# Pooled attention and a soft mixture of experts on one core: fewer and longer idle products on TensorE, one more row group of w2 by halves, and the uneven rows moved from w2 to w1

## The chip, the core and the metric

The kernel runs on one core of one Trainium2 chip. The metric is the device time of one execution in microseconds (us); of several runs of a kernel the median is given. The page and the views quoted below come from one execution taken by the hardware profiler. Its span, from the first to the last instruction, is a little shorter than its time.

## The reference

What is computed is an attention over pooled keys and values, and behind it a soft mixture of experts on the attention's output:

```python
# q, k, v: (8, 8, 576, 64); phi: (512, 32); w1: (8, 512, 1024); w2: (8, 1024, 512); all float32
k_p = k.reshape(B, H, Sp, pool, D).mean(axis=3)         # pool = 8, Sp = 72
v_p = v.reshape(B, H, Sp, pool, D).mean(axis=3)
attn = softmax(scale * np.matmul(q, k_p.transpose(0, 1, 3, 2)))
x = np.matmul(attn, v_p)                                # as (4608, 512)
logits = x @ phi
slot_input = softmax(logits, axis=0).T @ x              # 32 slots, 4 for each of 8 experts
for e in range(E):
    slot_out[e] = np.maximum(slot_input[e] @ w1[e], 0.0) @ w2[e]
out = softmax(logits, axis=1) @ slot_out                # (4608, 512)
```

## The kernel before

The batch is worked in four pairs of two. For each pair the kernel pools k and v with products against a constant matrix, turns q, forms the scores, exponentiates them on ScalarE (ACT) and multiplies by v extended by v times phi, so that x and the logits come out together. These stages are interleaved by hand; each engine runs its instructions in the order in which the code writes them. When the fourth pair is done, the slots' inputs are there, and the experts follow: `hidden()` (w1), `turn_hidden()`, and `second_layer()` (w2, which adds up in one PSUM tile, `so_ps`). Then every tile of 128 rows of the output is one product with `so` (`product()`), scaled by ACT or VectorE (DVE) in `put()` and stored from SyncE (SP) in `store()`.

All inputs but a part of k come in through DMAs that GpSimd (POOL) issues, with a cast from float32 to bfloat16 on the way. POOL issues them in the order in which the code writes them, and the order in which they land is that one: q, k, v of the pairs, with w1 (`load_w1`, L103) between them from the second pair on, then w2 (`load_w2`, L109; L458 and L459), and at last the pieces of L482. Sizes in the views of the DMA are those of the destination, in bfloat16.

Of the experts' w2, experts 0 to 5 are loaded in whole rows. Of expert 6 (`E - 2`) the first `CUT6` = 4 of its 8 row groups (a row group: 128 rows, one on each partition, 512 columns) come in whole rows, 8 KB of float32 on each partition, by L459; this load is cut by partitions into 0 to 112, 112 to 120 and 120 to 128, so that it is three DMAs. The remaining 4 groups of expert 6 and the 8 of expert 7 are loaded by halves of the columns (L477 to L485): first the left 256 columns of all of these groups in the four pieces of `PIECES` (L92), then the right 256 columns. So the left half of the output can be begun (`begin(0)`, L632) before the right half of these weights is there.

While TensorE (PE) waits for w2, it runs products whose result nobody reads: `busy(n)` (L556) writes n products of 512 bfloat16 columns into `idle_ps`. The calls stand at L626 to L631: 6 before expert 6's whole rows, 3 behind them, and 3 and 2 behind the first two pieces of the left half. `row_sums()` (L393) forms the divisors of the output rows with ten products, a copy by ACT, four float32 transposes (L404) and two reciprocals by DVE (L405, L406).

The first product of the left half's output is L586; it needs the last piece of the left half. The output's tiles are stored in groups of 2, 2, 2, 4, 6, 8 and 12 rows on each partition; tiles 0 to 9 by halves of the columns, the last three groups in whole rows of 12, 16 and 24 KB on each partition.

Of the kernel before, what the change touches and what calls it, by code (L numbers as in the profile page):

```python
# [8 lines left out]
FP = mybir.dt.float32  # L9
# [9 lines left out]
def kernel(  # L19
# [10 lines left out]
    nc = tc.nc  # L30
# [4 lines left out]
    DM = H * D  # L35
    E = moe_w1.shape[0]
# [11 lines left out]
    DJ = DM // 128  # L48
    FJ = F // 128
# [21 lines left out]
    xsa = persist.tile([128, 2, 9 * H * XW], BF)  # L71
    exa = persist.tile([128, 2, 2, HQ, 2, S // 2], BF)
    w1_sb = persist.tile([128, E, DJ, F], BF)
    cT = persist.tile([128, 2, B * S // 2], BF)
# [11 lines left out]

    CUT6 = FJ - 4
    HC = DM // 2  # L90
    halves = [slice(0, HC), slice(HC, DM)]
    PIECES = ((E - 2, CUT6, FJ), (E - 1, 0, 4), (E - 1, 4, FJ - 1), (E - 1, FJ - 1, FJ))  # L92

    loaded = 0

    def load(src, pair):
        nonlocal loaded
        loaded += 1
        t = big[:, loaded % 4]
        nc.gpsimd.dma_start(out=t, in_=pair_of(src, pair))  # L100
        return t.rearrange("p (t d) -> p t d", d=D)

    def load_w1(e, n):  # L103
        nc.gpsimd.dma_start(out=w1_sb[:, e:e + n].rearrange("p e j f -> p e (j f)"),
                            in_=moe_w1[e:e + n].rearrange("e (p j) f -> p e (j f)", j=DJ))

    w2_at = {}

    def load_w2(home, e, n, j0=0, j1=FJ, parts=((0, 128),)):  # L109
        for i in range(n):  # L110
            for j in range(j0, j1):
                w2_at[e + i, j] = home[:, i, j * DM:(j + 1) * DM]
        src = moe_w2[e:e + n].rearrange("e (p j) d -> p e j d", j=FJ)[:, :, j0:j1].rearrange("p e j d -> p e (j d)")
        for p0, p1 in parts:
            nc.gpsimd.dma_start(out=home[p0:p1, 0:n, j0 * DM:j1 * DM], in_=src[p0:p1])


    CUT = 4 * POOL * D
# [8 lines left out]
    ident = consts.tile([128, 128], BF)  # L127
# [32 lines left out]
    with tc.tile_pool(name="tmp", bufs=1) as tmp:  # L160
# [39 lines left out]
    def after_k(p):  # L200
        if p + 1 < NP:
            q_sb[p + 1] = load(q, p + 1)
        if p == 1:
            load_w1(0, 1)

    def after_q(p):
        if p + 1 < NP:
            v_sb[p + 1] = load(v, p + 1)
        if p == 1:
            load_w1(1, 1)  # L210
        if p == 2:
# [37 lines left out]
    def prepare_kq(pair):  # L249

        means = kvpool.tile([128, NR, 2, D], BF, name="kmeans")
        yield from pool_stage(k_sb[pair], means, lambda: after_k(pair))
        kp[pair] = kvpool.tile([128, BH, SP], BF, name="kp", bufs=2)
        dst = kp[pair].rearrange("p n (r i) -> p r n i", r=NR)
        yield from turn_stage(means, lambda r0, r1, ps: nc.vector.tensor_copy(out=dst[:, r0:r1], in_=ps))
        for n, t0 in enumerate(range(0, NU, 6)):
            ps = ps_m.tile([128, 6, BH, NI], BF, name="q_ps", tag="m")
            for t in range(6):
                tt = 2 * (t0 + t)
                nc.tensor.transpose(out=ps[:, t].rearrange("p n i -> p (n i)"),  # L260
                                    in_=q_sb[pair][:, tt:tt + 2, :].rearrange("p t d -> p (t d)"), identity=ident)
            dst = qT[pair][:, :, t0:t0 + 6, :].rearrange("p n t i -> p t n i")
            if n % 3 == 1:
                nc.scalar.copy(out=dst, in_=ps)  # L264
            else:
                nc.vector.tensor_copy(out=dst, in_=ps)  # L266
            if n == NU // 6 - 1:
                after_q(pair)
            yield
# [123 lines left out]
    def row_sums():  # L393

        ps = ps_m.tile([NC, 4, 128], FP, name="R_ps", tag="m")
        for c, (_, t) in enumerate(quads + rest):
            nc.tensor.matmul(out=ps[:, 0:2 * t.shape[1]].rearrange("p (s r) i -> p s r i", r=2), 
                             lhsT=onehot[:, MAXC - 1 - c:MAXC - 1 - c + NC], rhs=t,
                             start=(c == 0), stop=(c == NC - 1), skip_group_check=True)
        sums = consts.tile([NC, 4, 128], FP)  # L400
        nc.scalar.copy(out=sums, in_=ps)
        ps = ps_m.tile([128, 4, NC], FP, name="RT_ps", tag="m")
        for i in range(4):
            nc.tensor.transpose(out=ps[:, i], in_=sums[:, i], identity=identf[0:NC, 0:NC])  # L404
        nc.vector.reciprocal(out=recR[:, 0:2], in_=ps[:, 0:2])  # L405
        nc.vector.reciprocal(out=recR[:, 2:4, 0:len(quads)], in_=ps[:, 2:4, 0:len(quads)])  # L406
# [21 lines left out]
    for pair in range(NP):  # L428
        for qd in range(2):
# [24 lines left out]
            if qd == 1:  # L454
                for _ in prep or ():
                    pass
            last = (pair, qd, ex)
    load_w2(qTa, 4, 2)  # L458
    load_w2(xsa[:, 0:1], E - 2, 1, 0, CUT6, ((0, 112), (112, 120), (120, 128)))  # L459

    u_tile(*last[:2], 4, last[2], by_scalar=True)
    G_ps = ps_m.tile([128, DM], FP, name="G_ps", tag="m")
# [6 lines left out]
    def half_home(e, half):  # L469
        if e == E - 1:  # L470
            flat = xsa[:, 1, half * FJ * HC:(half + 1) * FJ * HC]
        else:
            c0 = CUT6 * DM + half * (FJ - CUT6) * HC
            flat = xsa[:, 0, c0:c0 + (FJ - CUT6) * HC]
        return flat.rearrange("p (j c) -> p j c", c=HC)

    w2_half = {}  # L477
    for half, cols in enumerate(halves):
        for e, j0, j1 in PIECES:
            home = half_home(e, half)  # L480
            i = 0 if e == E - 1 else CUT6
            nc.gpsimd.dma_start(out=home[:, j0 - i:j1 - i],  # L482
                                in_=moe_w2[e].rearrange("(p j) d -> p j d", j=FJ)[:, j0:j1, cols])
# [44 lines left out]
    def second_layer(e, j0=0, j1=FJ, half=None):  # L528
        cols = slice(0, DM) if half is None else halves[half]
        for fj in range(j0, j1):  # L530
            g = fj % NG
            nc.tensor.matmul(out=so_ps[g * NS:(g + 1) * NS, cols], lhsT=hT[:, e, fj],  # L532
                             rhs=w2_at[e, fj] if half is None else w2_half[e, fj, half],
                             start=(e == 0 and fj < NG), stop=(e == E - 1 and fj >= NG), skip_group_check=True)
# [18 lines left out]

    idle = ps_m.tile([128, 512], FP, name="idle_ps", tag="m")

    def busy(n):  # L556
        for _ in range(n):
            nc.tensor.matmul(out=idle, lhsT=ident, rhs=cT[:, 0, 0:512], start=True, stop=True)  # L558

    def scaled(engine, dst, src, by):  # L560
        if engine == 0:
# [9 lines left out]
    n = 0  # L571
    places = []
    for rows, base in GROUPS:
        home = out_a[:, n:n + rows] if n + rows <= 6 else out_b[:, n - 6:n - 6 + rows]
# [25 lines left out]
    def begin(half):  # L600

        cols = halves[half]
        scaled(0, so_a[:, cols], so_ps[:, cols], recC)
        f0 = product(0, cols, True)
        second_layer(E - 1, J7, FJ, half)
        f1 = product(1, cols, True)
        put(0, cols, 0, f0)
        store(0, 0, 1, cols)
        scaled(1, so[:, cols], so_ps[:, cols], recC)
        put(1, cols, 0, f1)  # L610
        store(0, 1, 2, cols)
# [9 lines left out]
    for e in range(4):  # L621
        second_layer(e)
    row_sums()
    for e in range(4, E - 2):
        second_layer(e)
    busy(6)  # L626
    second_layer(E - 2, 0, CUT6)
    busy(3)
    for (e, j0, j1), n in zip(PIECES[:-1], (3, 2, 0)):
        second_layer(e, j0, j1, 0)  # L630
        busy(n)  # L631
    begin(0)  # L632
    tiles(2, 3, 0)
    tiles(3, 4, 0)
# [11 lines left out]
    for n in range(10, len(TILES)):  # L646
        g, r = TILES[n]
# [33 lines left out]
```

## Time and profile before

| | us |
|---|---|
| median of 3 runs | 177.48 (177.26 to 177.49) |
| the profiled execution, its time | 177.27 |
| its span | 175.5 |
| PE busy | 126.8 |
| DVE busy | 93.1 |
| ACT busy | 88.0 |
| POOL busy | 19.0 |

How to read the views. In a row of a timeline stand the start, the length, the engine, the line of the code, the operation, output and inputs by the program's names with their shapes, how many instructions the row groups, and in brackets the idle time of the engine before them with what ended it. PEld is TensorE's load of weights, which overlaps its products (PE). `POOLq` and `SPq` are these engines' queues of instructions. A row of windows gives a stretch and its length, then the busy time of PE, PEld, DVE, ACT and POOL with the number of instructions, the share of the clock that the throttle granted TensorE, the mean busy share of the 16 DMA engines by the packets that start in the stretch (over 1 where packets overlap), and the GB/s that they moved, by the destination's size. A row of a DMA queue has packets, MB, and the time of the packets as a share of 16 engines over the stretch asked for. A row of a DMA issue has the size and the median time from issue to landing.

### The profile page before, as it was taken

To read this page: it belongs to the slowest core of one execution; us is meant where nothing else is said; L and a number is where in the kernel's file an instruction comes from. 1 tells how busy PE (TensorE), PEld (TensorE's weight loads), DVE (VectorE), ACT (ScalarE), POOL (GpSimd) and SP (SyncE) were. 2 spreads that over 40 slices of the span, in tenths; PEclk is the share of its full clock that TensorE was granted. 3 is DMA by queue.
4 is the path that set the end of the run, shared out by engine and by line. 5 is a ranking of instruction groups with operands and counts; after the bars stand their busy time and mean duration, and the time that the engine had idled before them with its cause. 6 is when DMAs were issued, how large, how long until landed. Compare 5 with 4: busy or idle time off the path is not lost.

```text
span 175.5 us, 2874 instructions
## 1 busy us (share of the span) xinstructions
PE 126.8 (72%) x1119; PEld 68.9 (39%) x1119; DVE 93.1 (53%) x257; ACT 88.0 (50%) x168; POOL 19.0 (11%) x36
## 2 busy tenths in 40 slices
PE   0005787999899999999999897459968598795000
PEld 0002443665556655556655455323531233331000
DVE  5403344497868588795897758603540005698000
ACT  3201249884987649877399952440201006896000
POOL 7000111022110040000010024003010140000000
PEclk9999999999999999999999997557999789999555
DMA  5999999999999999999999999999999999999991
GB/s 196 245 210 225 218 210 216 220 212 222 207 218 218 211 227 206 220 212 215 220 220 211 213 217 222 215 213 213 222 217 213 196 195 216 309 395 439 463 387 73
DMA packets 10381, 41.14 MB, mean 234 GB/s; under 512 B 752, under 2 KB 6384, under 8 KB 6656
## 3 DMA queue, kind: packets, MB, share of 16 engines
q0 software_dynamic: 7040, 30.48, 85.4%
q1 hardware_dynamic: 3328, 10.49, 15.4%
q8 instruction: 9, 0.15, 0.3%
q14 instruction: 4, 0.03, 0.0%
HBM read 61.93 MB, written 9.44 MB: 407 GB/s over the span
## 4 chain that ended last, share of the span: by engine, by line
PE 35%; DMA 26%; issue 11%; ACT 11%; DVE 7%; POOL 1%; DVEq 0%; ACTq 0%; POOLq 0%
DMA qTa<-in_moe_w_dram 19%; PE pool_ps L228 9%; DMA phi_f<-in_moe_phi_dram 7%; PE q_ps L260 5%; PE sc L300 4%; ACT exa L302 4%; DVE w_sb L564 4%; PE u_ps L314 4%; PE idle_ps L558 2%; ACT vmeans L234 2%; PE G_ps L336 2%; PE so_ps L532 2%; PE turn_ps L244 2%; PE f_ps L589 1%; PE lg_ps L332 1%
## 5 line engine op out<-in xcount | busy, mean ns | idle before, releaser
L302 ACT ACTIVATE exa<-sc 72x576 bf16<-72x576 f32 x64 | 39.4, 653 | 4.6 <-PE sc L300 3.9
L325 DVE TENSOR_TENSOR xsa<-u_ps,rec 128x384 bf16<-128x384 f32 x69 | 37.5, 554 | 1.3
L314 PE MATMUL u_ps<-vp,exa 72*128 72x97 bf16 (+1 forms) x320 | 27.2, 218 | 4.2 <-DVE xsa L325 3.3
L314 PEld LDWEIGHTS <-exa 72*128 72x128 bf16 (+1 forms) x320 | 18.4, 105 | 15.1 <-DVE xsa L325 6.4
L300 PE MATMUL sc<-qTa,kp 64*72 64x288 bf16 x128 | 21.4, 302 | 1.9 <-ACT exa L302 1.5
L228 PE MATMUL pool_ps<-big,pmat 128*128 128x512 bf16 x64 | 18.1, 403 | 0.7 <-ACT qTa L264 0.6
L319 DVE RECIPROCAL rec<-u_ps 128x4 f32<-128x4 f32 x72 | 11.5, 173 | 12.5 <-PE u_ps L314 12.4
L180 PE MATMUL phi_ps<-spread,sel 128*128 128x256 bf16 x4 | 1.3, 394 | 15.0 <-DVE spread L175 15.0
L260 PE MATMUL q_ps<-ident,big 128*128 128x128 bf16 x144 | 11.6, 219 | 0.8 <-DVE qTa L266 0.3
L589 PE MATMUL f_ps<-so,cT 128*128 128x512 bf16 (+1 forms) x42 | 10.2, 337 | 1.8 <-ACT w_sb L562 0.8
L336 PE MATMUL G_ps<-xsa,ee 128*128 128x512 bf16 x36 | 10.2, 438 | 1.2 <-ACT ee L333 1.2
L300 PEld LDWEIGHTS <-kp 64*72 64x72 bf16 x128 | 7.9, 107 | 8.2 <-issue 3.1
L564 DVE TENSOR_SCALAR w_sb<-f_ps,recR 128x512 f32<-128x512 f32 (+1 forms) x17 | 10.5, 681 | 0.3
L236 DVE TENSOR_REDUCE rsum<-rest_ps 128x64 f32<-128x512 f32 x8 | 5.5, 692 | 8.6 <-PE rest_ps L232 8.5
L264 ACT COPY qTa<-q_ps 128x768 bf16<-128x768 bf16 x8 | 6.4, 795 | 7.0 <-PE q_ps L260 7.0
L260 PEld LDWEIGHTS <-big 128*128 128x128 bf16 x144 | 8.7, 97 | 2.9 <-issue 1.3
L562 ACT ACTIVATE w_sb<-f_ps,recR 128x512 f32<-128x512 f32 (+1 forms) x17 | 9.6, 639 | 0.4 <-PE f_ps L589 0.2
L266 DVE COPY qTa<-q_ps 128x768 bf16<-128x768 bf16 x16 | 8.8, 552 | 1.7 <-PE q_ps L260 1.6
L482 POOL DMA_DIRECT2D xsa<-in_moe_w_dram x8 | 5.7, 713 | 30.7 <-PE G_ps L336 11.4
L228 PEld LDWEIGHTS <-pmat 128*128 128x128 bf16 x64 | 5.8, 102 | 6.4 <-issue 2.4
L234 ACT CAST vmeans<-pool_ps 128x1024 bf16<-128x1024 f32 x4 | 4.0, 1012 | 6.8 <-PE pool_ps L228 6.8
L292 ACT CAST vp<-v_ps 72x384 bf16<-72x384 f32 x16 | 7.1, 488 | 0.1
(101 smaller groups left out, 147.4 us busy)
## 6 DMA issues: line engine op xcount, KB each, us to landing
w_sb<-in_moe_w_dram POOLq DMA_DIRECT2D x2, 3072.0 KB, 37.8
big<-in_q_dram POOLq DMA_DIRECT2D x4, 1152.0 KB, 12.7
big<-in_v_dram POOLq DMA_DIRECT2D x4, 1152.0 KB, 16.6
big<-in_moe_w_dram POOLq DMA_DIRECT2D x1, 4096.0 KB, 40.8
big<-in_k_dram POOLq DMA_DIRECT2D x3, 1152.0 KB, 21.3
out_dram<-w_sb SPq DMA_DIRECT2D x1, 3072.0 KB, 12.6
w_sb<-in_moe_w_dram POOLq DMA_DIRECT2D x2, 1024.0 KB, 19.4
qTa<-in_moe_w_dram POOLq DMA_DIRECT2D x1, 2048.0 KB, 33.9
```

What stands on the lines that cost most here:

```text
L228: nc.tensor.matmul(out=ps, lhsT=pmat, rhs=src[:, t:full * POOL:POOL, :], start=(t == 0), stop=(t == POOL - 1))
L260: nc.tensor.transpose(out=ps[:, t].rearrange("p n i -> p (n i)"), in_=q_sb[pair][:, tt:tt + 2, :].rearrange("p t d -> p (t d)"), identity= ...
L266: nc.vector.tensor_copy(out=dst, in_=ps)
L300: nc.tensor.matmul(out=ps[:, r, 0:S // 2], lhsT=kp[pair][rows, n], rhs=qT[pair][rows, n].rearrange("p t i -> p (t i)"), start=True, stop=True)
L302: nc.scalar.activation(out=dst.rearrange("p r (i t) -> p r i t", t=NU), in_=ps[:, :, 0:S // 2].rearrange("p r (t i) -> p r i t", i=NI), fu ...
L314: nc.tensor.matmul(out=ps[rows, hh], lhsT=ex[b][:, hh].rearrange("p r t -> p (r t)")[:, c:c + rows.stop - rows.start], rhs=vp[(2 * pair + ...
L319: nc.vector.reciprocal(out=rec, in_=ps[:, :, XW])
L325: nc.vector.tensor_tensor(out=dst, in0=ps[:, :, 0:XW], in1=rec.rearrange("p h -> p h ()").to_broadcast([128, HQ, XW]), op=ALU.mult)
L336: nc.tensor.matmul(out=ps, lhsT=ee[:, t].rearrange("p g s -> p (g s)"), rhs=x[:, t, :, 0:D], start=(t == 0), stop=(t == 8))
L562: nc.scalar.activation(out=dst, in_=src, func=AF.Copy, scale=by)
L564: nc.vector.tensor_scalar(out=dst, in0=src, scalar1=by, scalar2=None, op0=ALU.mult)
L589: nc.tensor.matmul(out=ps, lhsT=tokens(n), rhs=so[:, cols], start=True, stop=True)
```

## The change

Three things change.

1. `busy()` issues one float32 product instead of a row of bfloat16 ones. Its operands are `cT` read as float32 (the same bytes), 128 columns as weights and n columns as the moving operand. There are four calls where there were four calls of 14 products in all: 512 columns behind `row_sums()`, 512 before expert 6's whole rows, 256 before each of the first two pieces of the left half. Behind the second of these there is none.
2. `CUT6` becomes 3: expert 6 has three row groups in whole rows and five by halves, so that with the eight of expert 7 thirteen row groups come by halves instead of twelve. Its whole rows come in one DMA instead of three.
3. The cut by partitions (0 to 112, 112 to 120, 120 to 128) goes to the load of w1 of expert 0, which POOL issues in the second pair: the first 2560 of its 4096 elements on each partition (10 KB of float32) come in three DMAs, the rest in one.

```diff
-    CUT6 = FJ - 4
+    CUT6 = FJ - 5
...
-    def load_w1(e, n):
-        nc.gpsimd.dma_start(out=w1_sb[:, e:e + n].rearrange("p e j f -> p e (j f)"),
-                            in_=moe_w1[e:e + n].rearrange("e (p j) f -> p e (j f)", j=DJ))
+    UNEVEN = 2560
+
+    def load_w1(e, n, uneven=False):
+        dst = w1_sb[:, e:e + n].rearrange("p e j f -> p e (j f)")
+        src = moe_w1[e:e + n].rearrange("e (p j) f -> p e (j f)", j=DJ)
+        if uneven:
+            for p0, p1 in ((0, 112), (112, 120), (120, 128)):
+                nc.gpsimd.dma_start(out=dst[p0:p1, :, 0:UNEVEN], in_=src[p0:p1, :, 0:UNEVEN])
+            dst, src = dst[:, :, UNEVEN:], src[:, :, UNEVEN:]
+        nc.gpsimd.dma_start(out=dst, in_=src)
...
-    def load_w2(home, e, n, j0=0, j1=FJ, parts=((0, 128),)):
+    def load_w2(home, e, n, j0=0, j1=FJ):
...
-        for p0, p1 in parts:
-            nc.gpsimd.dma_start(out=home[p0:p1, 0:n, j0 * DM:j1 * DM], in_=src[p0:p1])
+        nc.gpsimd.dma_start(out=home[:, 0:n, j0 * DM:j1 * DM],
+                            in_=moe_w2[e:e + n].rearrange("e (p j) d -> p e j d", j=FJ)[:, :, j0:j1].rearrange("p e j d -> p e (j d)"))
...
         if p == 1:
-            load_w1(0, 1)
+            load_w1(0, 1, True)
...
-    load_w2(xsa[:, 0:1], E - 2, 1, 0, CUT6, ((0, 112), (112, 120), (120, 128)))
+    load_w2(xsa[:, 0:1], E - 2, 1, 0, CUT6)
...
+    cTf = cT.rearrange("p r u -> p (r u)").bitcast(FP)
+
     def busy(n):
-        for _ in range(n):
-            nc.tensor.matmul(out=idle, lhsT=ident, rhs=cT[:, 0, 0:512], start=True, stop=True)
+        nc.tensor.matmul(out=idle[:, 0:n], lhsT=cTf[:, 0:128], rhs=cTf[:, 0:n], start=True, stop=True)
...
     row_sums()
+    busy(512)
     for e in range(4, E - 2):
         second_layer(e)
-    busy(6)
+    busy(512)
     second_layer(E - 2, 0, CUT6)
-    busy(3)
-    for (e, j0, j1), n in zip(PIECES[:-1], (3, 2, 0)):
+    for (e, j0, j1), n in zip(PIECES[:-1], (256, 256, 0)):
+        if n:
+            busy(n)
         second_layer(e, j0, j1, 0)
-        busy(n)
```

More of the change, by code (lines that the diff above doesn't have):

```diff
@@ L112, in load_w2 @@
                 w2_at[e + i, j] = home[:, i, j * DM:(j + 1) * DM]
-        src = moe_w2[e:e + n].rearrange("e (p j) d -> p e j d", j=FJ)[:, :, j0:j1].rearrange("p e j d -> p e (j d)")
-        for p0, p1 in parts:
-            nc.gpsimd.dma_start(out=home[p0:p1, 0:n, j0 * DM:j1 * DM], in_=src[p0:p1])
+        nc.gpsimd.dma_start(out=home[:, 0:n, j0 * DM:j1 * DM],
+                            in_=moe_w2[e:e + n].rearrange("e (p j) d -> p e j d", j=FJ)[:, :, j0:j1].rearrange("p e j d -> p e (j d)"))
     CUT = 4 * POOL * D
```

## The prediction

> **What bounds the kernel now.** I read the page's shares and slices first, then the DMA view cut at the instruction queue's packets, then the end of the span.
>
> ```profile
> PE 126.8 (72%) x1119; PEld 68.9 (39%) x1119; DVE 93.1 (53%) x257; ACT 88.0 (50%) x168; POOL 19.0 (11%) x36
> DMA  5999999999999999999999999999999999999991
> q0 software_dynamic: 7040, 30.48, 85.4%
> q1 hardware_dynamic: 3328, 10.49, 15.4%
> q8 instruction: 9, 0.15, 0.3%
> ```
>
> No engine is full, but the DMA line stands at 9 from the second slice to the last but one: the 16 DMA engines carry the kernel. So an edit is worth what it takes from the DMA engines' work, from their pauses, or from the lateness of the last of them. Queue q8, which brings instructions, has only 9 packets of 0.15 MB / 9 = 16 KB. They matter because one packet lies on one of the 16 engines. Here are the ninth, in the DMA view of 160.3 to 161.3 us, then the last 4 us by windows, and the last store's issue and landing:
>
> ```profile
> q8 instruction: 1, 0.02, 5.5%
> ```
> ```profile
> 171.25:171.90 0.65, 0.00 (x0) 0.00 (x0) 0.00 (x0) 0.00 (x0) 0.00 (x0) 0.50 0.00 0
> 171.90:173.75 1.85, 0.00 (x0) 0.00 (x0) 0.00 (x0) 0.00 (x0) 0.00 (x0) 0.50 0.07 27
> 173.75:175.50 1.75, 0.00 (x0) 0.00 (x0) 0.00 (x0) 0.00 (x0) 0.00 (x0) 0.50 0.00 0
> ```
> ```profile
> 161.58 0.33 SPq L580 DMA_DIRECT2D out_dram<-w_sb  x1
> out_dram<-w_sb SPq DMA_DIRECT2D x1, 3072.0 KB, 12.6
> ```
>
> 5.5% of 16 engines over 1.0 us is 0.88 us of one engine. In the last rows no packet starts from 171.25 to 171.90, and from 171.90 to 173.75 the share is 0.07, one sixteenth: fifteen engines have begun their last row of the 3 MB store by 171.25, and one still has two to go. Each is 24,576 bytes; at that row's 27 GB/s, 0.91 us. So fifteen end by about 172.1 and the last at 173.75. The store lands at 161.58 + 12.6 = 174.2 and the span ends 1.3 later. **One engine is about 1.7 us late, and the kernel's end is that engine's.** The late engine is one of sixteen, as it would be if the ninth packet had held it up; the packet's own 0.88 is half of it, and the other half I put down to the store packets on either side of it. That is the step most worth doubting.
>
> **Part 1: rows of the TensorE program.** Windows from the start to the first, eighth and ninth q8 packet:
>
> ```profile
> 0.00:33.60 33.60, 15.54 (x115) 8.63 (x116) 12.88 (x43) 13.22 (x24) 5.08 (x14) 1.00 0.98 218
> 0.00:133.40 133.40, 104.38 (x1002) 60.60 (x1003) 79.67 (x232) 73.63 (x140) 16.25 (x32) 0.95 1.02 216
> 0.00:160.30 160.30, 126.42 (x1119) 68.88 (x1119) 91.89 (x256) 87.55 (x168) 19.04 (x36) 0.95 1.03 225
> ```
>
> PE and PEld have started 231 rows at the first packet and 2005 at the eighth: 2005/8 = 251 apiece, 65 bytes a row; I take it as 64 bytes and 256 rows. So q8 follows TensorE's program, and a packet comes when the sequencer, some rows ahead of the engine, passes a multiple of 256: 25 rows ahead at the first, 43 at the eighth. At the ninth all 2238 have started, 66 short of 2304. With leads of 25 to 43 it would be due at 2261 to 2279; it can come only because the sequencer has run into the last rows (drains, waits, branches). The program crosses its ninth boundary by a handful of rows.
>
> The diff takes 14 idle products (28 rows, a load and a product each) and adds 4 (8 rows); the row group moved to halves turns one product into two (2 rows): -28 + 8 + 2 = -18, so 2220. That the float32 product is one pair I take from the float32 transposes, four calls with four loads and four products:
>
> ```profile
> L404 PEld LDWEIGHTS RT_ps<-identf,sums x4: 133/137/138, 136.2 to 136.3; 10*128 10x128 f32 x4
> L404 PE MATMUL RT_ps<-identf,sums x4: 203/203/224, 136.2 to 136.4; 10*128 10x10 f32 x4
> ```
>
> With 18 rows less the boundary falls behind the end of the work and the ninth packet does not come, or after the last store. Worth: **-1.7** (bounds: 0, if it comes all the same; -1.85, the whole window). The other eight packets stay: the edits to this program all lie behind the eighth.
>
> [...]
>
> **Part 2: the idle products as time on PE.** PE's timeline, the POOL issue and landing of the fourth and the last half piece, and the granted clock in four stretches of one throttle step each:
>
> ```profile
> 136.17 0.41 PE L404 MATMUL RT_ps<-identf,sums 10*128 10x10 f32 x4 [0.67 <-ACT sums L401]
> 138.16 1.90 PE L532 MATMUL so_ps<-qTa,hT 128*32 128x512 bf16 x16 [1.58 <-DMA qTa<-in_moe_w_dram]
> 140.00 2.19 PE L558 MATMUL idle_ps<-cT,ident 128*128 128x512 bf16 x6
> 142.45 0.82 PE L558 MATMUL idle_ps<-cT,ident 128*128 128x512 bf16 x3
> 143.20 0.29 PE L532 MATMUL so_ps<-xsa,hT 128*32 128x256 bf16 x4
> 145.16 0.28 PE L586 MATMUL f_ps<-xsa,zT 128*128 128x256 bf16 x1
> ```
> ```profile
> 128.96 0.58 POOL L482 DMA_DIRECT2D xsa<-in_moe_w_dram  x1 [8.73 <-DVE recC L541]
> xsa<-in_moe_w_dram POOLq DMA_DIRECT2D x1, 64.0 KB, 15.8
> xsa<-in_moe_w_dram POOLq DMA_DIRECT2D x1, 64.0 KB, 6.5
> ```
> ```profile
> 127.85:131.26 3.41, 1.92 (x35) 1.00 0.99 207
> 134.68:138.09 3.41, 1.24 (x8) 1.00 0.98 202
> 138.09:141.50 3.41, 3.34 (x20) 0.50 1.26 194
> 141.50:144.92 3.42, 3.42 (x23) 1.00 1.45 195
> ```
>
> The first half's last piece lands at 128.96 + 15.8 = 144.76, but PE uses it at 145.16: the idle products make PE 0.4 late. A float32 product of 512 columns is in no row. From below: a bfloat16 one is (143.20 - 142.45)/3 = 0.25. From above, far off: 10 float32 columns take 0.41/4 = 0.10, so 512 would take 5.2. I take four times the nearer row, 1.0; the exact value matters little. After the landing of qTa at 138.1 PE has until 144.5 (part 3), 6.3 us; its own products need 1.9 (at half clock) + 0.4 + 3 x 0.3 = 3.2, and the new idle ones 512 + 256 + 256 columns, two prices. Up to 1.5 us each they fit. The first, behind row_sums(), has 136.6 to 138.16 before the wait on qTa, 1.5 again; if it waits for DVE to read RT_ps first, 1.1; behind it stands only the product that waits for qTa. So PE comes **on time, 0.4 earlier**.
>
> The clock: after a stretch with 1.24 us busy PE got 0.50 for the next, after one with 1.92 it kept 1.00. The first new product lifts 1.24 to 2.2, which should keep 138.09 to 141.50 at full clock and save PE time that it only waits away. But the stretch to 144.92, full now, falls to about 1.8.
>
> [...]
>
> **Part 3: one more row group by halves.** DMA rates over full rows and over half rows, then the pause at 149.5:
>
> ```profile
> 121.00:136.00 15.00, 12.48 (x138) 5.42 (x136) 5.58 (x13) 2.02 (x4) 0.58 (x1) 1.00 1.04 217
> 141.60:146.40 4.80, 4.44 (x31) 1.42 (x30) 0.01 (x1) 0.77 (x2) 1.31 (x2) 1.00 1.45 195
> ```
> ```profile
> 149.00:149.50 0.50, 0.18 (x1) 0.01 (x1) 0.12 (x1) 0.50 (x2) 0.00 (x0) 1.00 0.87 293
> 149.50:150.00 0.50, 0.37 (x2) 0.09 (x1) 0.00 (x0) 0.14 (x2) 0.00 (x0) 1.00 0.23 76
> 150.00:150.50 0.50, 0.44 (x3) 0.21 (x3) 0.28 (x1) 0.44 (x2) 0.00 (x0) 1.00 1.03 338
> ```
>
> A row group is 131 KB in SBUF: 0.60 us as full rows, 0.34 a half. Before the first half's last piece stand one full group less and one half more: it lands 0.27 earlier, 144.5. With part 2, the first half's chain (products, scaling, stores of tiles 0 to 9) starts 0.65 earlier. In all the loads take 2 x 0.34 - 0.60 = **+0.07**.
>
> What do 0.65 bring at the end? The DMA engines are saturated by stores from 150.0 on and pause only at 149.5 to 150 (share 0.23, 0.39 us lost) and a little before. Earlier stores fill that pause, but those that run earlier share the engines with the second half's loads, last landing 142.32 + 6.5 = 148.8, and delay them; and the six-row group, computed by DVE and ACT behind the second half, gets no earlier. Bounds: -0.4 (the pause gone) to +0.3 (the second half's loads later by half of the 0.65, nothing gained). I take **-0.2**.
>
> **Part 4: uneven rows and POOL's queue.**
>
> ```profile
> 34.96 0.53 POOL L100 DMA_DIRECT2D big<-in_q_dram  x1 [6.47 <-PE u_ps L314]
> 35.48 0.54 POOL L104 DMA_DIRECT2D w_sb<-in_moe_w_dram  x1
> 41.41 0.53 POOL L100 DMA_DIRECT2D big<-in_v_dram  x1 [5.39 <-PE q_ps L260]
> 138.41 0.74 POOL L482 DMA_DIRECT2D xsa<-in_moe_w_dram  x1 [8.87 <-DMA qTa<-in_moe_w_dram]
> ```
>
> The first w1 load becomes four issues: 3 x 0.54 = 1.6 us, inside the 5.39 that POOL waits before 41.41. Two issues go at 105. Waits such as the one at 138.41 fall on the landing of the DMA eight issues before (128.96: w2 of experts 0 to 3; 138.41: qTa); one issue more moves each on by one, so two half pieces go out earlier, into a queue that is full anyway: 0.
>
> The two pieces of 8 rows shift load between DMA engines; they do so now with 8 KB rows of w2, later with 10 KB rows of w1. If the same engines take them, each gets two rows 2 KB longer, 4 KB at 27 GB/s: 0.15 of work, at most 0.15 late or early in the loads: **0**, bounds +/-0.15.
>
> **Sum** against the profiled execution (span 175.5, time 177.27): 177.27 - 1.7 - 0.2 + 0.07 = 175.4. The median of the runs, 177.48, is 0.2 above that execution, so I say **175.5**.
>
> **Rivals.**
> 1. *The packet still comes*: the float32 product takes more rows than its call (four pairs each would make 2220 + 24 = 2244, over 2238), or the boundary lies lower. [...] Against: the x4 rows, and the 66. Time 177.48 - 0.2 + 0.07 = 177.3. Chance 0.14.
> 2. *The late engine was late for another reason*, and the packet's own 0.88 is all that goes: 176.4. For: half of the lateness has no row. Chance 0.06.
> 3. *The clock falls* in 144.92 to 148.3, because the stretch before it holds 1.8 us where 3.42 are now. The first half's six steps each get about 0.1 to 0.2 longer, the 0.2 of part 3 is lost and up to 0.5 paid: 175.7 to 176.2. Chance 0.10.
> 4. *Slower*: the float32 idle products outlast the waits they fill. From 1.5 us per 512 columns each further us makes PE two us later at the first half; at 5.2 the three behind qTa take 10.4, PE comes 7 us late, and beyond about 2 us, when the second half is held up as well, the end moves with it: 177.48 - 1.7 + 5 = 180.8. Slower than before from about 3.3 us a product. Against: the bfloat16 row of the same shape is 0.25. Chance 0.04.
>
> **How the numbers follow.** The forecast (packet gone, 175.0 to 175.9) has 0.66. A measurement here can tell about 0.2%, 0.35 us. Faster: forecast, rivals 2 and 3, and a little of rival 1: 0.84. Same: most of rival 1, 0.11. Slower: 0.05. The forecast's range with rivals 2 and 3 holds 0.82: 174.9 to 176.5.
>
> **What would show it.** Right: q8 has 8 packets on the page; the last windows have no stretch with a share of one engine; PE and PEld count 1110 each; L586 first starts at about 144.5. Wrong: a ninth q8 packet between 133 and 172; 1122 or more rows each; a product of 512 float32 columns over 1.5 us; a pause of the DMA engines between 150 and 156, which would eat part 3; a last engine late without a q8 packet, which would overthrow part 1.

## The result and the profile after

The changed kernel takes **175.83 us**, the median of four runs (175.54 to 176.37), against 177.43 (177.26 to 177.49) of the kernel before beside it: a ratio of 0.9915, 95% interval 0.9889 to 0.9941. The forecast was 175.5, within 174.9 to 176.5. The profiled execution took 175.54, its span is 173.8; before they were 177.27 and 175.5. (Medians below hold all runs of a kernel; the ratios leave out runs over 1.5% above its fastest.)

The page after, in the lines that answer to those of before:

```profile
PE 127.8 (74%) x1114; PEld 69.1 (40%) x1114; DVE 93.1 (54%) x257; ACT 88.5 (51%) x168; POOL 19.9 (11%) x37
DMA  5999999999999999999999999999999999999994
q8 instruction: 8, 0.13, 0.3%
```

q8 has eight packets, not nine, and the last slice of the DMA line has grown from 1 to 4: the span now ends close behind the full slices. The same end in windows, then the last store's issue and landing:

```profile
171.25:171.90 0.65, 0.00 (x0) 0.00 (x0) 0.00 (x0) 0.00 (x0) 0.00 (x0) 0.50 0.01 0
171.90:173.75 1.85, 0.00 (x0) 0.00 (x0) 0.00 (x0) 0.00 (x0) 0.00 (x0) 0.50 0.00 0
```
```profile
161.52 0.33 SPq L587 DMA_DIRECT2D out_dram<-w_sb  x1
```
```profile
out_dram<-w_sb SPq DMA_DIRECT2D x1, 3072.0 KB, 10.8
```

The stretch in which one engine worked alone (share 0.07 from 171.90 to 173.75) is empty. The store is issued at 161.52, 0.06 before its time in the kernel before, and lands after 10.8 us where it took 12.6: at 172.3 in place of 174.2. **Nearly all of the gain lies between the issue of the last store and its landing**; what the change did to the work ahead of it moved that issue by 0.06. The store before it, of 2 MB, is quicker too: 7.5 us to its landing, where it took 9.4.

PE's timeline after (start, length, what), up to the first output product:

```profile
138.58 0.41 PE L410 MATMUL RT_ps<-identf,sums 10*128 10x10 f32 x4 [0.67 <-ACT sums L407]
138.92 1.12 PE L565 MATMUL idle_ps<-cT 128*128 128x512 f32 x2
139.98 1.05 PE L538 MATMUL so_ps<-qTa,hT 128*32 128x512 bf16 x16
143.92 0.71 PE L538 MATMUL so_ps<-xsa,hT 128*32 128x256 bf16 x7
144.70 0.27 PE L593 MATMUL f_ps<-xsa,zT 128*128 128x256 bf16 x1
```

One call of 512 float32 columns stands as two products and holds PE from 138.92 to 139.98, 1.06 us. Here PE was 2.4 us later at RT_ps than before (138.58 against 136.17), so it did not wait for qTa, and the idle products end just as the last piece of the left half lands: L593 begins at 144.70, where L586 began at 145.16.

SP's stores, before and after (the rows are groups of issues):

```profile
146.61 2.66 SPq L580 DMA_DIRECT2D out_dram<-exa  x5
149.38 1.07 SPq L580 DMA_DIRECT2D out_dram<-w_sb  x2
150.50 2.50 SPq L580 DMA_DIRECT2D out_dram<-exa  x4
153.11 8.80 SPq L580 DMA_DIRECT2D out_dram<-w_sb  x4
```
```profile
146.00 2.65 SPq L587 DMA_DIRECT2D out_dram<-exa  x5
148.85 0.99 SPq L587 DMA_DIRECT2D out_dram<-w_sb  x2
150.38 2.45 SPq L587 DMA_DIRECT2D out_dram<-exa  x4
152.93 8.92 SPq L587 DMA_DIRECT2D out_dram<-w_sb  x4
```

In each block the first two rows are the left half's stores; the third row and the first issue of the fourth are the right half's; the other three are the groups of 6, 8 and 12 rows. The left half's stores begin 0.61 and 0.53 earlier, the right half's (third row) only 0.12, and the last group's issue 0.06. The windows of the changed kernel show where the 0.6 goes:

```profile
149.50:150.00 0.50, 0.43 (x3) 0.11 (x3) 0.00 (x0) 0.14 (x2) 0.00 (x0) 1.00 1.07 356
152.00:153.00 1.00, 0.99 (x5) 0.52 (x5) 0.87 (x3) 1.00 (x3) 0.00 (x0) 1.00 0.64 216
```

The pause at 149.5 (share 0.23 before) is filled, and a new one of 0.36 us stands at 152 (the share there was 1.01 before), ahead of the right half's last store, which is issued at 152.93 (153.11 before). The group of six rows behind it is issued at 154.93, where it was at 154.99.

### The profile page after: what moved, and what is told of

The parts are those of the page before. It is cut to its first block, busy times and chain, and to the rows that moved or that the text cites. A ratio compares the mean times of both kernels' runs of the same rounds, so it can differ in the third digit from the quotient of the medians.

```text
span 173.8 us, 2869 instructions
## 1 busy us (share of the span) xinstructions
PE 127.8 (74%) x1114; PEld 69.1 (40%) x1114; DVE 93.1 (54%) x257; ACT 88.5 (51%) x168; POOL 19.9 (11%) x37
## 4 chain that ended last, share of the span: by engine, by line
PE 47%; ACT 18%; DMA 12%; DVE 11%; issue 3%; POOL 1%; DVEq 0%; ACTq 0%; POOLq 0%
PE pool_ps L234 10%; ACT exa L308 8%; DMA phi_f<-in_moe_phi_dram 7%; PE G_ps L342 6%; PE sc L306 6%; PE u_ps L320 6%; DMA xsa<-in_moe_w_dram 6%; PE q_ps L266 5%; DVE w_sb L571 4%; DVE xsa L331 3%; PE lg_ps L338 3%; ACT vmeans L240 2%; PE R_ps L403 2%; PE h_ps L517 2%; PE turn_ps L250 2%
## 5 line engine op out<-in xcount | busy, mean ns | idle before, releaser
L306 PE MATMUL sc<-qTa,kp 64*72 64x288 bf16 x128 | 21.9, 309 | 1.9 <-ACT exa L308 1.5
L234 PE MATMUL pool_ps<-big,pmat 128*128 128x512 bf16 x64 | 18.6, 411 | 0.7 <-ACT qTa L270 0.6
L325 DVE RECIPROCAL rec<-u_ps 128x4 f32<-128x4 f32 x72 | 11.5, 173 | 12.8 <-PE u_ps L320 12.7
L342 PE MATMUL G_ps<-xsa,ee 128*128 128x512 bf16 x36 | 11.5, 481 | 1.2 <-ACT ee L339 1.2
(102 smaller groups left out, 147.1 us busy)
## 6 DMA issues: line engine op xcount, KB each, us to landing
out_dram<-w_sb SPq DMA_DIRECT2D x1, 3072.0 KB, 10.8
```

Of the source, the lines that this page charges most:

```text
L234: nc.tensor.matmul(out=ps, lhsT=pmat, rhs=src[:, t:full * POOL:POOL, :], start=(t == 0), stop=(t == POOL - 1))
L306: nc.tensor.matmul(out=ps[:, r, 0:S // 2], lhsT=kp[pair][rows, n], rhs=qT[pair][rows, n].rearrange("p t i -> p (t i)"), start=True, stop=True)
L325: nc.vector.reciprocal(out=rec, in_=ps[:, :, XW])
L342: nc.tensor.matmul(out=ps, lhsT=ee[:, t].rearrange("p g s -> p (g s)"), rhs=x[:, t, :, 0:D], start=(t == 0), stop=(t == 8))
```

## The experiments

Two things were to be told apart. **First**, why the last engine was late: the theory is the ninth packet of instructions; the rivals are another cause (then a packet given back costs its own 0.9 us or nothing) and the loads. **Second**, what the other edits do: a clock that falls behind the idle products, and the loads' own effect. The kernels ran in three lots, four kernels to a chip, each lot beside the kernel before: its median was 177.45 in the first (35 runs), 177.59 in the second (23), 177.52 in the third (30).

### The rows given back

Behind the last output product of the changed kernel:

```diff
+    for _ in range(6):
+        nc.tensor.matmul(out=idle[:, 0:2], lhsT=ident, rhs=cT[:, 0, 0:2], start=True, stop=True)
```

> The changed kernel with six idle products of two columns behind the last product of the output (twelve rows of TensorE's program, whose results nobody reads). They stand where PE has nothing left to do, so no product of the output moves; the program is again as long as the one before. Theory (the ninth instruction packet makes one DMA engine 1.7 us late at the end): q8 has 9 packets again, the last about 160 us; one engine ends about 1.7 us behind the others, and the time is 177.2 to 177.6, that of before less 0 to 0.3. Rival (only the packet's own 0.88 us): 176.6 to 176.9. Rival (the gain came from the idle products or the loads): 175.5 to 176.4, as without the six, with or without a ninth packet.

Measured: 178.16 (177.78 to 179.63, 12 runs), ratio 1.0044 (1.0018 to 1.0069): the whole gain is gone, with six products of two columns each that nothing waits for. The time is above the expected 177.6 too, and 0.7 above the kernel before; more on that below. Its page, the end in windows, and the last two stores, from issue to landing:

```profile
PE 127.6 (72%) x1120; PEld 69.6 (40%) x1120; DVE 93.1 (53%) x257; ACT 88.2 (50%) x168; POOL 19.9 (11%) x37
q8 instruction: 9, 0.15, 0.3%
```
```profile
172.40:174.25 1.85, 0.00 (x0) 0.00 (x0) 0.00 (x0) 0.00 (x0) 0.00 (x0) 0.50 0.06 27
```
```profile
out_dram<-w_sb SPq DMA_DIRECT2D x1, 3072.0 KB, 12.7
out_dram<-w_sb SPq DMA_DIRECT2D x1, 2048.0 KB, 9.4
```

The ninth packet is back, and with it the one engine that starts two more rows when the others have started their last. The stores take 12.7 and 9.4 us again, as in the kernel before, where the changed kernel has 10.8 and 7.5. All the profiles on record agree: with nine packets (three of them) the last store takes 12.6 to 12.7 us, with eight (eleven of them) 10.7 to 10.9. What the queues start around that packet, first from 163.75 to 164.00, then from 164.36 to 164.60 (packets, MB, their time as a share of 16 engines):

```profile
q1 hardware_dynamic: 15, 0.25, 229.4%
```
```profile
q1 hardware_dynamic: 15, 0.25, 239.3%
q8 instruction: 1, 0.02, 24.3%
```

24.3% of 16 engines over 0.24 us is 0.93 us for the packet; 229.4% over 0.25 us for 15 rows is 0.61 for a row of 16 KB. In both stretches only 15 rows of the store are begun, and none between the two: the sixteenth engine begins nothing at 163.8. It is still in a row that began at 163.42. That row, and likewise the first one behind the packet, at 165.34, read in a view of 0.15 us around its start:

```profile
q1 hardware_dynamic: 1, 0.02, 41.9%
```

That is 1.01 us where such a row takes 0.61. So the engine loses 0.40 in the row ahead of the packet, 0.93 in the packet and 0.40 in the row behind it, in sum 1.73. In the trace of before a row of 12 KB (at 158.96, the last but one ahead of the packet) takes 0.92 instead of 0.46, the packet 0.88, and the row of 16 KB behind it 1.02 instead of 0.61: in sum 1.75. Why the rows on either side are slow, no row shows. All of this lies in the store of 2 MB, ahead of the last one. Rival 2 of the prediction falls.

In this profile (177.88, against 177.27 before) most of what puts the time above the kernel before lies ahead of the packet: the last store is issued at 162.01, 0.43 later, behind a step of the clock at 0.50 from 146.3 to 149.7, among the output's products. Before had such a step from 138.1 to 141.5, ahead of them. That this step is the cause is argued from the one pair, not shown.

### The new idle products alone

The kernel before, its loads untouched, with the changed kernel's `busy()` and its four calls:

```diff
-        for _ in range(n):
-            nc.tensor.matmul(out=idle, lhsT=ident, rhs=cT[:, 0, 0:512], start=True, stop=True)
+        nc.tensor.matmul(out=idle[:, 0:n], lhsT=cTf[:, 0:128], rhs=cTf[:, 0:n], start=True, stop=True)
```

> The kernel before with the new idle products alone: loads, row groups by halves and uneven rows as before. Theory: it has 12 rows less than before (two pairs for each float32 product), q8 has 8 packets, and the time is 175.5 to 176.1: all of the gain but the 0.1 to 0.2 that the row group by halves brought. Rival (row group and w1 rows matter as much): 176.5 or more.

Measured: 176.16 (175.23 to 177.76, 12 runs), ratio 0.9931 (0.9897 to 0.9964). The last store, in a profiled execution of 176.52:

```profile
out_dram<-w_sb SPq DMA_DIRECT2D x1, 3072.0 KB, 10.7
```

No engine is late and q8 has eight packets. The whole gain comes without any edit of the loads, and its six lowest runs are 175.23 to 175.79, where the lowest of the changed kernel on the same chip (12 runs, below) is 175.79.

### The changed kernel with even rows

```diff
-            load_w1(0, 1, True)
+            load_w1(0, 1)
```

> The changed kernel with all rows even: w1 of expert 0 in one DMA, nothing cut by partitions. Theory (uneven rows shift at most 0.15 us in the loads): 175.7 to 176.1, no difference that can be measured from the changed kernel (175.83). Rival (the eight instruction packets before the end of the loads make eight engines 0.9 us late, and the uneven rows give the others two rows more; without them the last engine's loads end later): the last load lands 0.3 to 0.4 later than 149.0, and the time is 176.1 to 176.3.

Measured: 176.35 (175.49 to 178.79, 12 runs), ratio 0.9916 (0.9883 to 0.995). Beside the changed kernel on the same chip (176.95, below) it is not slower, rather a little faster; the intervals overlap. Its last load lands at 149.5, 0.4 to 0.5 later than in the changed kernel's three profiles, as the rival has it; but with twelve row groups (last lot) even rows land at 148.7 and uneven ones at 149.2, so the rival is not shown.

### The changed kernel again

No edit.

> The changed kernel once more, for the spread of its runs (175.54 to 176.37 in four) and a second profile. Theory: the throttle's steps of 3.4 us lie differently in each execution, PE reaches the second layer up to 2.5 us earlier or later, and the new first idle product then stands before or behind the landing of qTa; the first product of the left half starts between 144.4 and 145.2, and times lie between 175.4 and 176.4. Rival: the spread is in the start or in the stores, and L593 starts at the same time in all profiles.

Measured: 176.95 (175.79 to 178.73, 12 runs), ratio 0.995 (0.9919 to 0.9982). By the medians 0.5 us of the first 1.6 are left, by the ratio 0.5% of 0.85%. Seven of the twelve runs lie above the 176.4 that was expected. Six runs, 175.79 to 176.65, had a mean granted clock of 0.911 to 0.923, the other six, 177.25 to 178.73, of 0.899 to 0.903. The profiled one is of the second kind (177.25). Its windows, cut at the steps in which the clock changes:

```profile
134.49:137.91 3.42, 2.36 (x10) 0.90 (x9) 0.40 (x2) 0.57 (x1) 0.00 (x0) 1.00 1.00 205
137.91:141.32 3.41, 2.73 (x23) 1.05 (x22) 0.00 (x0) 0.00 (x0) 1.13 (x2) 1.00 1.29 194
141.32:144.74 3.42, 1.91 (x16) 0.85 (x15) 0.00 (x0) 0.00 (x0) 0.22 (x1) 1.00 1.45 195
144.74:148.15 3.41, 3.10 (x17) 1.33 (x19) 1.56 (x4) 2.29 (x6) 0.00 (x0) 0.50 1.37 209
148.15:151.57 3.42, 3.14 (x19) 0.92 (x16) 1.18 (x3) 1.78 (x5) 0.00 (x0) 0.50 0.89 294
151.57:154.98 3.41, 3.31 (x12) 1.68 (x12) 2.28 (x6) 2.96 (x7) 0.00 (x0) 0.50 0.68 229
```

The first column of numbers behind the length is PE's busy time, the third from the end the clock. The step with 1.91 busy is followed by three at 0.50, to 154.98. In the execution of 175.54 the steps lie elsewhere, and those around the idle products are fuller:

```profile
140.06:143.47 3.41, 3.41 (x29) 1.24 (x30) 0.00 (x0) 0.00 (x0) 0.59 (x1) 1.00 1.45 195
143.47:146.88 3.41, 2.66 (x19) 1.30 (x20) 0.73 (x2) 1.56 (x4) 0.00 (x0) 1.00 1.44 194
```

The left half's first product begins only 0.11 later (144.70 there); what the half clock costs is seen behind it, in SP's stores of the slower execution:

```profile
144.81 0.37 PE L593 MATMUL f_ps<-xsa,zT 128*128 128x256 bf16 x1
```
```profile
146.23 2.90 SPq L587 DMA_DIRECT2D out_dram<-exa  x5
151.23 2.77 SPq L587 DMA_DIRECT2D out_dram<-exa  x4
154.15 9.50 SPq L587 DMA_DIRECT2D out_dram<-w_sb  x4
```

The left half begins 0.23 later than in the execution of 175.54, the right half 0.85, and the last issue ends at 154.15 + 9.50 = 163.65 in place of 152.93 + 8.92 = 161.85: 1.8 later, which is the whole difference of 1.7 between the two. The share of the DMA engines from 151.57 to 154.98 is 0.68, and PE is busy for 3.31 of these 3.41 us: the DMA engines wait for output. So the rival was right that the spread lies in the stores; the clock's steps set it, but behind the first product and not ahead of it.

### Fuller idle products

```diff
-    for (e, j0, j1), n in zip(PIECES[:-1], (256, 256, 0)):
+    for (e, j0, j1), n in zip(PIECES[:-1], (512, 512, 256)):
```

> The changed kernel with longer idle products: 512 columns instead of 256 before the first two pieces of the left half, and one more of 256 before the third (four rows more). Theory now: what is lost in about half of the changed kernel's executions (177.2 to 178 at a mean clock of 0.90, against 175.5 to 176.3 at 0.92) is the clock: a throttle step around 142 to 146 us with about 1.9 to 2.1 us of PE busy in 3.41 makes the next ones run at 0.50, in which the output's products lie. These products fill the waits between the pieces (0.3 to 0.7 each). So q8 keeps 8 packets, no step between 137 and 160 is at 0.50 in the profile, the median is 175.6 to 176.1, and at most 3 of 12 runs lie above 176.7. Rival (idle products make PE late): the first product of the left half starts after 145.3 and the median is 176.3 or more. Rival (the four rows bring the ninth packet back): 177.3.

Measured: 176.85 (175.64 to 179.68, 8 runs), ratio 0.9929 (0.9902 to 0.9957), and this count of rows:

```profile
PE 131.7 (74%) x1116; PEld 70.0 (39%) x1116; DVE 93.0 (53%) x257; ACT 88.2 (50%) x168; POOL 19.9 (11%) x37
q8 instruction: 8, 0.13, 0.3%
```

1116 products and loads, 2232 rows, still bring eight packets up to the end (a ninth begins at 178.1, behind the last store's landing at 175.7); 1119 (before) and 1120 (the rows given back) bring nine. Five of the eight runs took 175.64 to 177.00 at a mean granted clock of 0.924 to 0.935, where the highest of the changed kernel's 28 runs is 0.924; the ratio is that of these five. The other three took 179.04 to 179.68 at 0.895 to 0.905. The profiled execution is one of them (179.04):

```profile
141.11 0.41 PE L410 MATMUL RT_ps<-identf,sums 10*128 10x10 f32 x4 [0.67 <-ACT sums L407]
148.37 0.28 PE L593 MATMUL f_ps<-xsa,zT 128*128 128x256 bf16 x1
```

No step behind 130 us is at 0.50 here, as expected, but the clock was at 0.50 from 99.0 to 105.8 and from 112.6 to 129.7. So PE comes late to `row_sums()`, the idle products still stand ahead of the left half, and L593 begins 2.9 us after the last piece of the left half has landed (145.4). That is the rival that the idle products make PE late, and the median is over its 176.3. In five runs the clock is kept, but no time is won by it.

### Fuller, without the first

The edit above, and:

```diff
     row_sums()
-    busy(512)
```

> The same without the idle product behind row_sums(), so with as many rows as the changed kernel. Theory: the step that holds the wait for qTa falls to about 1.2 us of PE busy and the next, 138 to 141.5, runs at 0.50 as in the kernel before; that costs PE waiting time only, and the products behind it bring the clock back before the output's products: median 175.6 to 176.2, at most 3 of 12 above 176.7. Rival (the low step holds on into the output's products): half of the runs above 176.7.

Measured: 177.29 (175.74 to 178.44, 12 runs), ratio 0.9973 (0.9941 to 1.0005): the gain is all but lost, and nine of the twelve runs lie above 176.7, where three were expected at most. The profiled execution (177.52) shows how:

```profile
138.31 1.90 PE L538 MATMUL so_ps<-qTa,hT 128*32 128x512 bf16 x16 [2.20 <-DMA qTa<-in_moe_w_dram]
140.14 2.08 PE L565 MATMUL idle_ps<-cT 128*128 128x512 f32 x2
146.96 0.28 PE L593 MATMUL f_ps<-xsa,zT 128*128 128x256 bf16 x1
```

Without the first product PE stands 2.20 us ahead of qTa, the clock falls for 137.4 to 144.3, a call of 512 columns takes 2.0 in place of 1.06, and the left half starts 2.3 us late.

### No idle products

```diff
     row_sums()
-    busy(512)
...
-    busy(512)
     second_layer(E - 2, 0, CUT6)
-    for (e, j0, j1), n in zip(PIECES[:-1], (256, 256, 0)):
+    for (e, j0, j1), n in zip(PIECES[:-1], (0, 0, 0)):
```

> The changed kernel without any idle product. Theory: the clock is at 0.50 in the output's products in nearly all executions: median 177.0 to 178.0, at most 3 of 12 below 176.3, 8 packets on q8. Rival (idle products only delay PE): the median is 175.5 to 175.9, below the changed kernel's.

Measured: 176.78 (175.93 to 177.86, 12 runs), ratio 0.9946 (0.9918 to 0.9974), eight packets. The profiled execution (177.86):

```profile
135.33:138.75 3.42, 0.94 (x8) 0.50 (x6) 0.40 (x2) 0.57 (x1) 0.00 (x0) 1.00 1.00 200
138.75:142.16 3.41, 2.48 (x19) 0.75 (x19) 0.00 (x0) 0.00 (x0) 1.35 (x2) 0.50 1.37 193
152.40:155.81 3.41, 3.41 (x13) 1.66 (x12) 2.52 (x5) 2.99 (x7) 0.00 (x0) 0.50 0.68 226
```

A step with 0.94 busy is followed by half the clock, here to 155.8, and the mean clock is 0.881 to 0.901 in all twelve runs. The median lies between theory (177.0 to 178.0) and rival (175.5 to 175.9). Yet the ratio is that of the changed kernel in the other two lots (0.995 and 0.9961) within the intervals: over many runs the four float32 products win no time that could be measured here. That the fourteen are gone is what pays.

### The loads alone

The kernel before with parts 2 and 3 of the change alone, and its fourteen idle products:

```diff
-    CUT6 = FJ - 4
+    CUT6 = FJ - 5
...
-            load_w1(0, 1)
+            load_w1(0, 1, True)
...
-    load_w2(xsa[:, 0:1], E - 2, 1, 0, CUT6, ((0, 112), (112, 120), (120, 128)))
+    load_w2(xsa[:, 0:1], E - 2, 1, 0, CUT6)
```

> The loads of the changed kernel (thirteen row groups by halves, uneven rows in w1) with the fourteen bfloat16 idle products of the one before, so with its long program. Theory: 9 packets on q8, one engine 1.7 to 1.9 us behind at the end, and 177.1 to 177.6 as before (ratio 0.998 to 1.001); most runs keep the clock. Rival (the loads bring half of the gain): 176.6 or less.

Measured: 179.09 (178.16 to 180.11, 6 runs), ratio 1.0085 (1.0054 to 1.0116), well above the 177.1 to 177.6 that was expected. PE's timeline and the end of the profiled execution (180.11):

```profile
141.73 0.41 PE L410 MATMUL RT_ps<-identf,sums 10*128 10x10 f32 x4 [0.67 <-ACT sums L407]
147.59 0.28 PE L592 MATMUL f_ps<-xsa,zT 128*128 128x256 bf16 x1
```
```profile
174.50:176.35 1.85, 0.00 (x0) 0.00 (x0) 0.00 (x0) 0.00 (x0) 0.00 (x0) 0.50 0.06 27
```

The late engine is there again with its nine packets, and PE is 5.6 us later at RT_ps than in the profile of before: its clock was 0.50 from 99.6 to 106.4 and from 113.2 to 130.3, and the fourteen products, 3.7 us between the two rows shown, then make the left half later still (its last piece had landed at 144.7). Why all six runs lie above 178 is not settled: a low step that begins at 99 is in four of the nine profiles with uneven rows of w1 and in none of the five with even ones, which is too few to say that the loads set it.

### The loads, one by one

Four kernels in one lot, to settle the loads. First the kernel before with the new idle products, once more; then the changed kernel with twelve row groups by halves; then that one with even rows of w1 as well; last the changed kernel itself.

```diff
-    CUT6 = FJ - 5
+    CUT6 = FJ - 4
```
```diff
-    CUT6 = FJ - 5
+    CUT6 = FJ - 4
...
-            load_w1(0, 1, True)
+            load_w1(0, 1)
```

> The kernel before with the new idle products alone, for the second time, now beside its neighbours in the loads. Theory A (the load edits cost a little): 0.3 to 0.6 us below the changed kernel, about 175.9. Theory B (they are neutral, and only the phase of the clock's steps makes the medians differ): within 0.3 us of it. Theory C (part 3 of the prediction): 0.1 us above it.

> The changed kernel with twelve row groups by halves instead of thirteen, its uneven rows of w1 kept. Theory A, if the thirteenth row group is what costs: about 175.9, as the run with before's loads; if the uneven rows cost: as the changed kernel, 176.3 to 176.9. Theory B: within 0.3 us of the changed kernel. Theory C: 0.1 us above it, with the left half's first output product at about 145.1 us in place of 144.7.

> The changed kernel with twelve row groups by halves and no DMA cut by partitions, in w1 or in w2. Theory A: 0.3 to 0.6 us below the changed kernel, the best of the four. Theory B: within 0.3 us of it. Theory C: 0.1 us above it.

> The changed kernel again, as the measure of the other three on this chip. All theories: 175.5 to 176.0 in the executions without a low step of the granted clock behind 138 us, 176.6 to 177.6 in the others, 8 packets of instructions in both; the median falls by which of the two is the commoner on this chip.

| loads | us (range, runs) | ratio to before |
|---|---|---|
| of before | 176.00 (175.26 to 177.28, 6) | 0.9882 (0.9835 to 0.993) |
| twelve groups, uneven w1 | 176.37 (175.78 to 178.22, 12) | 0.9932 (0.9896 to 0.9967) |
| twelve groups, all even | 176.46 (175.5 to 177.92, 12) | 0.9927 (0.9895 to 0.9959) |
| of the changed kernel | 176.95 (175.89 to 178.75, 12) | 0.9961 (0.9925 to 0.9998) |

Theory C, the gain of part 3, has nothing for it: all three stand below the changed kernel. Theories A and B are not fully told apart. Before's loads were 0.95 lower here and 0.79 lower in the first lot, and the means of the lowest three runs 0.32 and 0.56; but the intervals overlap. With nine packets on both sides the kernels with the changed loads were above the kernel before as well, by 0.7 (the rows given back) and 1.5 (the loads alone), and there the intervals lie above 1. All this points to a small cost of the load edits, but neither edit taken back alone returned it. The best version of all the kernels, by its medians in both lots, is the one with before's loads and the new idle products.

Nine profiled executions without a ninth packet (those of the two kernels with fuller products are left out) stand roughly in the order in which the low steps of the clock behind 138 us end. That any such step costs, as the last expectation had it, is not so: the 175.89 of the third lot has one, to 149.0.

| execution | low steps, us | last store lands | us |
|---|---|---|---|
| changed kernel, first | none until 163.9 | 172.3 | 175.54 |
| changed kernel, third lot | 145.5 to 149.0 | 172.7 | 175.89 |
| even rows | 146.5 to 149.9 | 173.3 | 176.45 |
| twelve groups, uneven | 146.9 to 150.3 | 173.0 | 176.46 |
| before's loads, third lot | 146.4 to 153.2 | 172.9 | 175.99 |
| before's loads, first lot | 147.1 to 154.0 | 173.4 | 176.52 |
| twelve groups, even | 144.5 to 154.8 | 173.8 | 176.97 |
| changed kernel, first lot | 144.7 to 155.0 | 174.1 | 177.25 |
| no idle products | 138.8 to 155.8 | 174.7 | 177.86 |

## Why the prediction was right, and where it was not

**Part 1, the packet: right, and the step "most worth doubting" holds.** The ninth packet went, and the end came 1.85 us earlier at the store's landing (1.7 were forecast). Given back by twelve rows that do nothing, it makes the last store take 12.7 us again instead of 10.8. The packet's own time is half of it; the other half is a slow row ahead of the packet and one behind it, 0.40 to 0.46 each, as the trace of before already held and the prediction took it. One figure was wrong without harm, and that is luck: the float32 transposes of L404 are one pair each, but a float32 product is two pairs (eight loads and eight products for the four calls), so the program shrank by 10 rows of the trace (1114 pairs), not 18. The rounding of the 251 rows counted for a packet, and the sequencer's run into the last rows, were the author's estimate, and no run shows them to the row; what the runs show is that the boundary lies between 2232 rows (eight packets) and 2238 (nine): three to five more pairs, and rival 1, whose premise came half true (two pairs, not four), would have been the outcome.

**Part 2, the idle products: the price was right, the clock's was not.** 512 float32 columns take 1.06 us at full clock; 1.0 was taken, a choice of the author's between the bounds of 0.25 and 5.2, which no row of before shows. The first product behind `row_sums()` does what was said: the step that held 1.24 busy holds 2.36 in the changed kernel's second profile, and the next one keeps 1.00; without it, with 0.94, the next one is at 0.50. That PE is on time also came out, though in the first profile by another way: PE was 2.4 late, with low steps at 99 to 106 and 113 to 123 (before: 107 to 121), and never waited for qTa. **Rival 3 is the part that was mis-sized.** It said that the stretch to 144.92 falls to 1.8 busy and the clock falls behind it, at a price of up to 0.5 and a chance of 0.10. Measured in the second profile are 1.91, and then three steps at 0.50 instead of one. Half of the changed kernel's runs in the first and the third lot, six of twelve each, have the low mean clock (0.905 or less) that goes with it, and the price is up to 1.7. The prediction priced the left half's steps alone; the steps of the right half and of the group of six lie behind them, at half clock too, and the last store waits for that group. That the first four runs show none of it (0.917 to 0.923) is luck: the result met the forecast more closely than the kernel does, whose median over all its 28 runs is 176.51, at the upper end of the range.

**Part 3, the row group by halves: -0.2 was too much.** The chain did start 0.46 earlier, and the stores 0.61, but the last store only 0.06. What the prediction named as proof against itself, a pause between 150 and 156, is there at 152. Its own sentence, that the six-row group gets no earlier, was the answer: that group's store moved by 0.06 (154.99 to 154.93), and so did the last one. The left half's gain ends there, and the term should have been priced at that. The last piece of the left half lands 0.1 earlier rather than 0.27 (144.66 against 144.76): qTa itself landed 0.3 later in this execution. The experiments on the loads show no gain at all.

**Part 4, the uneven rows: 0 was taken, +/-0.15.** Even rows were 0.60 lower in the first lot and 0.09 higher (with twelve groups) in the third, both within the intervals. Whether the uneven ones cost something stays open.

**The sum.** 177.27 less 1.85 for the packet is 175.42; the measured 175.54 leaves +0.1 for all the rest, where -0.13 was forecast. Rival 4 fell with the 1.06, rival 2 with the rows given back.

## What to carry to other kernels

A DMA engine that ends alone is worth tracing back to the one packet it had more than the others. Here a program that was a few rows longer (2238 rows instead of 2232 or fewer) brought one more packet of instructions into the stores, which cost the end 1.85 us; filler instructions count as rows (six products of two columns were enough). Work that started earlier paid here only as far as the last store's issue moved (0.06, where the first stores moved by 0.61): read that row first. Where the clock goes by steps (of 3.41 us here), one profile shows one phase of them: judge a filler by a dozen runs with it and a dozen without, not by the step that it fills in one profile.

## What the runs showed that was not expected

**The clock's phase.** Its steps are 3.41 us long, and their phase differs from one execution of the same kernel to the next: the table has low steps from 144.7, from 145.5 and from 163.9 for the changed kernel. Steps with 0.94, 1.91 and, in the third lot's profile of the changed kernel, 2.10 us of PE busy were followed by 0.50:

```profile
142.16:145.57 3.41, 2.10 (x18) 0.88 (x13) 0.00 (x0) 0.59 (x2) 0.00 (x0) 1.00 1.45 196
145.57:148.98 3.41, 3.31 (x23) 1.43 (x22) 1.97 (x5) 2.16 (x5) 0.00 (x0) 0.50 1.29 246
```

Steps at full clock with 2.36 to 3.41 in the rows above kept 1.00. But the busy share alone does not decide: a step with 1.92 kept it in a row of the prediction, and in the changed kernel's first profile the step from 95.65 to 99.06, with 2.79 us of PE busy, was followed by 0.50. What else decides is open. In the traces of before and of the changed kernel's first profile the granted clock is 1.00 or 0.50 and nothing between; and of the steps above that were followed by 0.50, three were more than half busy (1.91, 2.10 and 2.79 of 3.41).

**The mean clock and the time.** Of 52 runs of the changed kernel and of the two with twelve groups, the 29 up to 176.81 us had a mean granted clock of 0.911 or more, and of the 23 from 176.92 on all but one (177.17 at 0.912) had 0.905 or less. So a median of a few runs mixes two kinds, and a change of the mixture looks like a change of the kernel. The mixture did change: in the lots, 12 of the changed kernel's 24 runs have a mean clock of 0.905 or less, and 24 of the 88 of the kernel before one of 0.908 or less. Among the runs with the higher clock the medians are 176.02 and 177.43, 1.4 apart, which is most of the packet's price; among those with the lower clock they are 177.72 and 178.61. Why the changed kernel has the lower clock more often is not settled.
